# The attention half of a sketched-attention and expert-layer kernel, rebuilt

## The chip, the core and the metric

The kernel runs on one core of a Trainium2 chip. A core has the matrix engine TensorE (PE, with its weight loads shown apart as PEld), VectorE (DVE), ScalarE (ACT), GpSimd (POOL) and a queue SyncE (SP) that issues DMAs; they run side by side and meet at semaphores. The metric is device microseconds of one execution, the median of several. All arithmetic is fp32; each fp32 matmul shows in the trace as two pairs of a weight load (LDWEIGHTS) and a MATMUL, a transpose as one pair.

## What is computed

```python
# q, k, v: (B, H, S, D) = (4, 4, 1088, 32); S1, S2: (r, D) = (8, 32), float64 on arrival
def phi(x):
    a = np.einsum('rd,bhsd->bhsr', S1, x)
    b = np.einsum('rd,bhsd->bhsr', S2, x)
    return np.einsum('bhsi,bhsj->bhsij', a, b).reshape(*x.shape[:-1], r * r)
q_p, k_p = phi(q), phi(k)
kv  = np.einsum('bhsf,bhsd->bhfd', k_p, v);   z = np.sum(k_p, axis=2)
x   = np.einsum('bhsf,bhfd->bhsd', q_p, kv) / (np.einsum('bhsf,bhf->bhs', q_p, z)[..., None] + 1e-06)
x   = x.transpose(0, 2, 1, 3).reshape(4352, 128)            # one row per token
logits = x @ w_gate                                         # 8 experts
e_idx  = argmax(logits); gate_w = softmax(logits)[e_idx]; eom = sigmoid(x @ w_output_gate)
out[t] = gate_w[t] * eom[t, e] * (relu(x[t] @ w1[e]) @ w2[e])     # e = e_idx[t], 128 -> 1024 -> 128
```

## The kernel before

Tokens lie in 34 chunks of 128, and chunks in nine groups of four (the last has two). The work has two halves.

**Attention and routing.** For a group of keys, `ab` (L253) multiplies each chunk and pair of heads with both sketches: the chunk of `kT` is the stationary operand (128 columns), `S12blk` the moving one (32 columns). The sketches arrive as float64 and are held as a high and a low fp32 part, so `kT` and `qT` are loaded twice, once for each part, into partitions 0 to 63 and 64 to 127. ScalarE copies the b half out of PSUM (L256) and VectorE forms all products a·b (`kp`, L259). `kvs` (L280) sums `kp` against `vt` over the tokens of one batch entry, 65 moving columns (64 values and a one for z); `fin` (L266, L269) masks the result into `kz`. A batch entry has 1088 tokens, 8.5 chunks, so some chunks are split. For a group of queries, `fa` and `fb` (L298) compute features times tokens directly with 512 moving columns, ScalarE copies one (L305), VectorE multiplies (L310), `nd` (L318) multiplies with `kz` (66 moving columns: numerators and denominators), VectorE divides (L321 to L325), and `logits` transposes x (L333) and multiplies with the gate matrix (L338, 16 moving columns). `route` (L357 to L400), once a group, finds the winning expert, counts places with two matmuls (L372, L373), forms the gate weight, and then GpSimd writes each chunk's rows with one scatter (L400) to the place of its expert in the DRAM array `xs`: 34 scatters. The order of this half comes from a scheduler that places instructions by their dependences. At its end GpSimd writes one scatter of padding rows (L446), and VectorE makes a table of the 41 tiles of 128 rows (L451 to L484).

**Experts.** Each of the 41 tiles is read back from `xs` (L496), transposed (L507), multiplied up (L516) and down (L526) with the weights of its expert, scaled and scattered to the output (L529). This half has an order written by hand and is not touched. Its first read must wait until all scatters into `xs` have landed.

PSUM tiles come from rings: "t" and "w2" have two buffers each, "kvz" and "rt" one.

Of the kernel before, what the change touches and what calls it, by code (L numbers as in the profile page):

```python
# [2 lines left out]

# [8 lines left out]
F32 = mybir.dt.float32  # L12
# [18 lines left out]
def kernel(  # L31
# [52 lines left out]
    rows = consts.tile([2 * r, 128], F32, tag="rows")  # L84
    bits = consts.tile([2 * r, 64, 2], I32, tag="bits")
    if not wide:
        nc.vector.memset(rows, 0.0)
    for i, x in enumerate((S1, S2)):
        own = slice(i * r, (i + 1) * r)
        if wide:  # L90
            x, dst, n = x.bitcast(I32), bits[own].rearrange("p (h d) w -> p h (d w)", h=2), 2 * D
        else:
            dst, n = rows[own, :64].rearrange("p (h d) -> p h d", h=2), D
        nc.sync.dma_start(dst, bass.AP(tensor=x.tensor, offset=x.offset, ap=[[n, r], [0, 2], [1, n]]))
    wg = consts.tile([DM, 2 * E], F32, tag="wg")
    nc.sync.dma_start(wg, wg_d)
# [3 lines left out]
    kT = consts.tile([128, 2, N], F32, tag="kT")  # L100
    qT = consts.tile([128, 2, N], F32, tag="qT")
# [6 lines left out]
    def load_T(dst, src, g):  # L108
        cs = groups[g]
        for i in range(2):  # L110
            nc.sync.dma_start(dst[64 * i:64 * (i + 1), :, cols(cs)],
                              src[:, cols(cs)].rearrange("(a p) n -> p a n", a=2))

    def load_k(g):
        cs = groups[g]
        load_T(kT, kT_d, g)
# [3 lines left out]
    def load_q(g):  # L120
        load_T(qT, qT_d, g)
# [12 lines left out]
    lead = need[0] + 1  # L134
    for g in range(lead):
        load_k(g)
# [16 lines left out]
    make_identity(nc, ident)  # L153
    ones = consts.tile([128, 128], F32, tag="ones")
# [8 lines left out]
    nc.vector.tensor_scalar(efirst, eio, -1.0, float(E), op0=ALU.mult, op1=ALU.add)  # L163
    ecap = consts.tile([128, E], F32, tag="ecap")
    nc.vector.tensor_scalar_mul(ecap, eio, float(CAP))
# [16 lines left out]
    nc.vector.tensor_copy(padoff, padoff_i)  # L182
    padcap = consts.tile([128, E], F32, tag="padcap")
    nc.vector.tensor_scalar_mul(padcap, eio, float(CAP - PP * PR))
# [5 lines left out]
    nc.vector.tensor_copy(step, step_i)  # L190
    stepT = consts.tile([128, max(NT, KN)], F32, tag="stepT")
    nc.vector.tensor_scalar_mul(stepT, step, float(TS))  # L192
# [5 lines left out]
    def split():  # L198
# [3 lines left out]
        sign, ex, mant, low, scale = (consts.tile([2 * r, 64], I32, tag=f"bit{i}", name=f"bit{i}") for i in range(5))  # L202
# [11 lines left out]
        nc.vector.tensor_copy(rows[:, :64], mant.bitcast(F32))  # L214
        nc.vector.tensor_copy(rows[:, 64:], low)
        nc.vector.tensor_mul(rows[:, 64:], rows[:, 64:], scale.bitcast(F32))
    if wide:
        split()

    ps = ps_t("ps_rows")  # L220
    nc.tensor.transpose(ps[:, :2 * r], rows, ident[:2 * r, :2 * r])
    S12T = consts.tile([128, 2 * r], F32, tag="S12T")
    nc.vector.tensor_copy(S12T, ps[:, :2 * r])

    mask2 = consts.tile([128, 2], F32, tag="mask2")
    maskh = consts.tile([128, 2], F32, tag="maskh")
    nc.vector.memset(maskh, 0.0)
    for h in range(2):
        nc.vector.memset(maskh[64 * h:64 * (h + 1), h:h + 1], 1.0)
    nc.vector.memset(mask2, 0.0)  # L230
    for i in range(4):
        nc.vector.memset(mask2[i * D:(i + 1) * D, i % 2:i % 2 + 1], 1.0)

    S12blk = consts.tile([128, 2, 2 * r], F32, tag="S12blk")
    nc.vector.tensor_mul(S12blk, bview(S12T, [[0, 2], [1, 2 * r]]), bview(mask2, [[1, 2], [0, 2 * r]]))
# [5 lines left out]


    kvz_done, acc = {}, {}

    def k_steps(g):
        cs, s = groups[g], {}
        n = len(cs) * H
# [345 lines left out]
```

## Time and profile before

| | us |
|---|---|
| median of three runs | 307.65 (306.43 to 311.29) |
| the profiled execution's own time | 307.44 |
| its span, first to last instruction | 305.7 |
| PE busy, PEld busy | 265.9, 243.1 |
| DVE, POOL, ACT busy | 103.3, 77.5, 57.5 |

A busy time counts the stretch in which an engine has at least one instruction in flight. Matmuls are pipelined, so the time from one start to the next says more than the length of one. The chain of waits is followed back from the last instruction to what released each step; the table of stages gives the busy time of each engine in chosen stretches.

### The profile page before, as it was taken

How to read it: one execution, taken by the hardware profiler on the slowest of the kernel's cores; microseconds unless marked ns; L12 is line 12 of the kernel's file. 1: busy time of each engine (PE TensorE's matmuls, PEld its weight loads, DVE VectorE, ACT ScalarE, POOL GpSimd, SP SyncE). 2: the span in 40 equal slices, each digit the busy share in tenths (PEclk: the TensorE clock that was granted, in tenths of full speed). 3: DMA queues.
4: the chain of work that ended last, by engine and by line, in shares of the span. 5: the costliest groups of instructions: out<-in, count | busy, mean ns of one | idle time of the engine just before them, and what ended most of it. 6: DMA issues, size and time to landing. Idle time of an engine off the chain costs nothing.

```text
span 305.7 us, 5829 instructions
## 1 busy us (share of the span) xinstructions
PE 265.9 (87%) x1990; PEld 243.1 (80%) x1990; DVE 103.3 (34%) x402; ACT 57.5 (19%) x108; POOL 77.5 (25%) x108
## 2 busy tenths in 40 slices
PE   0997979999999988402999999999999999999980
PEld 0996557787786657402999999999999999999980
DVE  5202115555665655761222222222222222222200
ACT  1000102121122121100122222222222222222220
POOL 4000000235135134770022222222222222222230
PEclk9999979899999999655899999999999999999997
DMA  5999999601011001112158488878783288751000
GB/s 137 248 239 248 238 240 294 246 26 35 2 36 38 9 27 37 45 56 76 35 171 260 152 242 244 253 234 288 208 288 116 71 247 244 233 201 37 17 2 0
DMA packets 22062, 44.50 MB, mean 146 GB/s; under 512 B 3642, under 2 KB 9532, under 8 KB 22032
## 3 DMA queue, kind: packets, MB, share of 16 engines
q1 hardware_dynamic: 19488, 39.10, 45.6%
q0 software_dynamic: 2544, 5.03, 4.8%
q8 instruction: 16, 0.26, 0.4%
q14 instruction: 14, 0.11, 0.1%
HBM read 60.06 MB, written 5.48 MB: 214 GB/s over the span
## 4 chain that ended last, share of the span: by engine, by line
issue 39%; PE 35%; POOL 13%; DVE 4%; DMA 3%; POOLq 1%; ACT 1%; SPq 1%; ACTq 0%
POOL out_dram L529 12%; PE ps_kvz L280 7%; PE ps_ab L253 6%; PE ps_fa L298 6%; PE ps_nd L318 6%; PE ps_fb L298 4%; PE ps_l L338 3%; DMA kT<-in_k_dram 1%; DMA xs<-pad,pai 1%; PE ps_xt L333 1%; POOLq L529 1%; PE ps_pos L372 1%; DVE kp L259 1%; DMA xin<-xs 1%; PE ps_pos L373 1%
## 5 line engine op out<-in xcount | busy, mean ns | idle before, releaser
L516 PE MATMUL ps_h<-xsT,wt 128*128 128x128 f32 x656 | 81.8, 279 | 0.0
L526 PE MATMUL ps_y<-wt,hT 128*128 128x128 f32 x656 | 79.8, 275 | 0.0
L516 PEld LDWEIGHTS ps_h<-xsT,wt 128*128 128x128 f32 x656 | 78.4, 196 | 0.0
L526 PEld LDWEIGHTS ps_y<-wt,hT 128*128 128x128 f32 x656 | 76.5, 192 | 0.0
L529 POOL DMA_INDIRECT out_dram<-y,xin x41 | 39.8, 971 | 122.0 <-ACT y L528 122.0
L400 POOL DMA_INDIRECT xs<-x,sloti x34 | 33.3, 981 | 98.2 <-DVE sloti L390 63.3
L509 DVE COPY xsT<-ps_xs 128x128 f32<-128x128 f32 x41 | 12.0, 292 | 86.8 <-PE ps_xs L507 86.8
L520 DVE TENSOR_SCALAR hT<-ps_h 128x1024 f32<-128x1024 f32 x20 | 24.5, 1225 | 30.1 <-PE ps_h L516 21.1
L518 ACT ACTIVATE hT<-ps_h 128x1024 f32<-128x1024 f32 x21 | 21.5, 1023 | 50.9 <-PE ps_h L516 28.7
L528 ACT ACTIVATE y<-ps_y,xin 128x128 f32<-128x128 f32 x41 | 15.1, 367 | 81.1 <-PE ps_y L526 81.1
L280 PEld LDWEIGHTS ps_kvz<-vt,kp 128*128 128x128 f32 (+1 forms) x144 | 23.5, 245 | 8.1 <-DVE kp L259 4.4
L280 PE MATMUL ps_kvz<-vt,kp 128*128 128x65 f32 (+1 forms) x144 | 24.0, 330 | 3.8 <-DVE kp L259 3.2
L507 PE MATMUL ps_xs<-ident,xin 128*128 128x128 f32 x41 | 11.7, 286 | 14.3 <-DMA xin<-xs 14.3
L253 PEld LDWEIGHTS ps_ab<-S12blk,kT 128*128 128x128 f32 x136 | 20.8, 241 | 2.6 <-DVE stepT L192 2.1
L253 PE MATMUL ps_ab<-S12blk,kT 128*128 128x32 f32 x136 | 20.9, 316 | 2.0 <-DMA kT<-in_k_dram 2.0
L298 PE MATMUL ps_fa<-qT,Sa 128*128 128x512 f32 (+1 forms) x36 | 21.9, 728 | 0.0
L318 PEld LDWEIGHTS ps_nd<-kz,qp 128*128 128x128 f32 (+1 forms) x144 | 16.7, 187 | 2.1 <-issue 1.5
L318 PE MATMUL ps_nd<-kz,qp 128*128 128x66 f32 (+1 forms) x144 | 18.1, 274 | 0.1
L259 DVE TENSOR_TENSOR kp<-ps_ab,b_sb 128x1024 f32<-128x1024 f32 (+1 forms) x9 | 10.5, 1165 | 22.3 <-ACT b_sb L256 20.2
L507 PEld LDWEIGHTS ps_xs<-ident,xin 128*128 128x128 f32 x41 | 6.0, 148 | 14.7 <-DMA xin<-xs 14.7
L298 PE MATMUL ps_fb<-qT,Sb 128*128 128x512 f32 (+1 forms) x36 | 16.9, 591 | 0.0
L310 DVE TENSOR_TENSOR qp<-a_sb,ps_fb 128x1024 f32<-128x1024 f32 (+1 forms) x9 | 10.4, 1160 | 12.1 <-PE ps_fb L298 11.6
(117 smaller groups left out, 146.6 us busy)
## 6 DMA issues: line engine op xcount, KB each, us to landing
wt<-in_w_dram SPq DMA_DIRECT2D x88, 512.0 KB
kT<-in_k_dram SPq DMA_DIRECT2D x16, 256.0 KB
qT<-in_q_dram SPq DMA_DIRECT2D x16, 256.0 KB
xin<-xs SPq DMA_DIRECT2D x41, 65.0 KB
vt<-in_v_dram SPq DMA_DIRECT2D x8, 260.0 KB
out_dram<-y,xin POOLq DMA_INDIRECT x41
xs<-x,sloti POOLq DMA_INDIRECT x34
kT<-in_k_dram SPq DMA_DIRECT2D x2, 128.0 KB
```

Source lines behind the costliest of these rows:

```text
L253: nc.tensor.matmul(ps[:, j * H + 2 * p:j * H + 2 * p + 2], kT[:, p, c * 128:(c + 1) * 128], S12blk, start=True, stop=True)
L280: nc.tensor.matmul(acc[b][:, p], s["kp"][p0:p0 + np_, j * H + 2 * p:j * H + 2 * p + 2].rearrange("s h i j -> s (h i j)"), vt[p0:p0 + np_, ...
L298: nc.tensor.matmul(ps[:, p, :n], S_.rearrange("p h i j -> p (h i j)"), qT[:, p, cols(cs)], start=True, stop=True)
L318: nc.tensor.matmul(ps[p0:p0 + np_, p, j], s["qp"][:, p, j * 128 + p0:j * 128 + p0 + np_], kvz_done[b][:, p], start=True, stop=True)
L400: apart("rows", nc.gpsimd.indirect_dma_start(out=xs[:, :], out_offset=bass.IndirectOffsetOnAxis(ap=sloti[:, j:j + 1], axis=0), in_=s["x"][ ...
L507: nc.tensor.transpose(ps, xin[t][:, :DM], ident)
L516: nc.tensor.matmul(ps[:, c], wt[t % NW][0][:, c], xT, start=True, stop=True)
L518: nc.scalar.activation(hTs[t], ps, ACTF.Relu)
L520: nc.vector.tensor_scalar_max(hTs[t], ps, 0.0)
L526: nc.tensor.matmul(ps, hT[:, c], wt[t % NW][1][:, c], start=(c == 0), stop=(c == FC - 1))
L528: nc.scalar.activation(y, ps, ACTF.Copy, scale=x[:, DM:DM + 1])
L529: apart("out", nc.gpsimd.indirect_dma_start(out=out, out_offset=bass.IndirectOffsetOnAxis(ap=x.bitcast(I32)[:, DM + 1:DM + 2], axis=0), in ...
```

## The change

The expert half stays. In the attention half:

- `kT` and `qT` hold each value once (128 rows: four heads of 32). The high and low parts of the sketches become two matmuls that add up in PSUM.
- Keys and queries go through the same `featured`: per chunk four matmuls with 64 stationary columns (half a chunk of tokens) and 64 moving ones, into the upper and the lower half of the PSUM partitions in turn; then the same copy and the same product as before for keys. `fa`, `fb` and L310 go.
- `sums` has one matmul for each head (64 stationary columns), halves in turn. `turned` transposes the query products, two transposes a chunk, and ScalarE copies them. `attend` has four matmuls a chunk with 64 stationary columns and 98 moving ones: the 66 of before and 32 more that hold `kz` times the gate matrix (`gates_T`, `gates`, once a batch entry). `shared` divides and adds up the logits on VectorE, so the transposes, matmuls and copies of `logits` go.
- Routing is done for eight chunks at once (`choose`, `place`, `send`): five times, of 8, 8, 8, 8 and 2 chunks. Places are counted with a scan; two small operations of it go to GpSimd. There are still 34 scatters and one of padding.
- The loads are issued as a list of 18 items: k0 k1 k2 q0 k3 q1 k4 q2 k5 q3 k6 q4 k7 q5 k8 q6 q7 q8. A loop over n = 0 to 21 writes out the order by hand: `featured` of item n, `place`, `sums` or `turned` of item n-1, `gates_T`, `attend` of item n-2, `gates`, `send`, `shared`, `choose`.
- Constants for routing are made on GpSimd instead of VectorE, and the gate matrix is loaded behind the first key group.

```diff
-    kT = consts.tile([128, 2, N], F32, tag="kT")
-    qT = consts.tile([128, 2, N], F32, tag="qT")
+    kT = consts.tile([128, N], F32, tag="kT")
+    qT = consts.tile([128, N], F32, tag="qT")
...
-        load_T(kT, kT_d, g)
+        nc.sync.dma_start(kT[:, cols(cs)], kT_d[:, cols(cs)])
...
+    items, made = [], 0
     for g in range(len(groups)):
-        load_q(g)
-        if lead + g < len(groups):
-            load_k(lead + g)
+        while made < len(groups) and made < max(need[g] + 1, need[0] + 1 + g):
+            items.append(("k", made))
+            made += 1
+        items.append(("q", g))
+    wg2 = consts.tile([2 * D, 2, 2 * E], F32, tag="wg2")
+    for i, (kind, g) in enumerate(items):
+        (load_k if kind == "k" else load_q)(g)
+        if i == 0:
+            nc.sync.dma_start(wg2, wg_d.rearrange("(s p) e -> p s e", s=2))
...
+    carry = consts.tile([128, E], F32, tag="carry")
+    nc.gpsimd.memset(carry, 0.0)
+    nc.gpsimd.tensor_copy(carry[0:1], ecap[0:1])
+    RG = 2 * GRP // 128
+    routes = [range(c, min(c + RG, NC)) for c in range(0, NC, RG)]
...
+    Sb = consts.tile([128, 2, H, 2 * r], F32, tag="Sb")
+    nc.vector.tensor_mul(Sb, bview(ps, [[2 * r, 2], [0, H], [1, 2 * r]]), bview(maskh, [[0, 2], [1, H], [0, 2 * r]]))
...
+    def featured(src, cs, name):
         n = len(cs) * H
+        ps = ps_t("ps_ab")[:, :4 * H * 2 * r].rearrange("p (a b) -> p a b", b=2 * r)
+        for j, c in enumerate(cs):
+            for i in range(2):
+                for t in range(2):
+                    nc.tensor.matmul(ps[64 * t:64 * (t + 1), j * H:(j + 1) * H],
+                                     src[:, c * 128 + 64 * t:c * 128 + 64 * (t + 1)], Sb[:, i],
+                                     start=i == 0, stop=i == 1, skip_group_check=True)
+        b_sb = work.tile([128, 4 * H, r], F32, tag="b_sb", name="b_sb")
+        nc.scalar.copy(b_sb[:, :n], ps[:, :n, r:])
+        res = work.tile([128, 4 * H, r, r], F32, tag=name, name=name)
+        av, bv = ps[:, :n, :r], b_sb[:, :n]
+        nc.vector.tensor_mul(res[:, :n], ...)
...
+    def gates_T(b):
+        ps = psum.tile([2 * D, 2, 128], F32, tag="rt", name="ps_kzT")
+        for s in range(2):
+            nc.tensor.transpose(ps[:, s], kz[b][:, s, :2 * D], ident)
+        kzT = work.tile([2 * D, 2, 128], F32, tag="kzT", name="kzT")
+        nc.scalar.copy(kzT, ps)
+        return kzT
+    def gates(b, kzT):
+        ps = psum.tile([128, 2, 4 * E], F32, tag="rt", name="ps_kg")
+        for s in range(2):
+            nc.tensor.matmul(ps[:, s], kzT[:, s], wgb[:, s].rearrange("p h e -> p (h e)"), start=True, stop=True)
+        nc.scalar.copy(kz[b][:, :, VZ:], ps)
+    def sums(cs, kp, todo):
...
+                for s in range(2):
+                    for h in range(2):
+                        nc.tensor.matmul(acc[b][64 * h:64 * (h + 1), s],
+                                         kp[p0:p0 + np_, j * H + 2 * s + h].rearrange("s i j -> s (i j)"),
+                                         vt[p0:p0 + np_, c, s], start=first and s == 0, stop=last, skip_group_check=True)
+                if last:
+                    close(b)
+                    todo.append(b)
+                    yield
+    def turned(cs, qp):
+        n = len(cs)
+        ps = ps_w("ps_qT").rearrange("p a (c x) -> p (a c) x", x=128)
+        for j in range(n):
+            for s in range(2):
+                nc.tensor.transpose(ps[:, 2 * j + s], qp[:, j * H + 2 * s:j * H + 2 * s + 2].rearrange("p h i j -> p (h i j)"), ident)
+        qpT = work.tile([128, 8, 128], F32, tag="qpT", name="qpT")
+        nc.scalar.copy(qpT[:, :2 * n], ps[:, :2 * n])
+        return qpT
+    def attend(cs, qpT):
+        ps = ps_w("ps_nd").rearrange("p a (c x) -> p (a c) x", x=128)
+        for j, c in enumerate(cs):
+            for s in range(2):
+                for t in range(2):
+                    nc.tensor.matmul(ps[64 * t:64 * (t + 1), 2 * j + s, :VG], qpT[:, 2 * j + s, 64 * t:64 * (t + 1)],
+                                     kz[(c * 128 + 64 * t) // S][:, s], start=True, stop=True)
+        return ps
+    def shared(cs, ps):
...
+        nc.vector.tensor_scalar_add(rc_, ps[:, :2 * n, 2 * D:VZ], EPS)
+        nc.vector.reciprocal(rc_, rc_)
+        nc.vector.tensor_mul(xts[i][:, at:at + n, :DM]..., ps[:, :2 * n, :2 * D]..., rc_...)
+        lg = work.tile([128, 8, 2, 2 * E], F32, tag="lg", name="lg")
+        nc.vector.tensor_mul(lg[:, :2 * n], ps[:, :2 * n, VZ:VG]..., rc_...)
+        nc.vector.tensor_reduce(Ls[i][:, at:at + n], lg[:, :2 * n]..., axis=AX, op=ALU.add)
...
+    def choose(i):
...
+        nc.vector.tensor_reduce(mx[:, :n], L, axis=AX, op=ALU.max)
+        nc.vector.tensor_tensor(ex[:, :n, :E], bc(mx), L, op=ALU.subtract)
+        nc.vector.scalar_tensor_tensor(out=t8[:, :n], ...)
+        nc.vector.tensor_reduce(first[:, :n], t8[:, :n], axis=AX, op=ALU.max)
+        nc.scalar.copy(oh[:, :, 0], state["carry"])
+        nc.vector.tensor_tensor(oh[:, :, 1:]..., t8[:, :n], bc(first), op=ALU.is_equal)
+        nc.vector.tensor_tensor_scan(cum..., fresh[n]..., oh..., 0.0, op0=ALU.mult, op1=ALU.add)
+    def place(i, oh, cum):
+        pp = psum.tile([128, E, RG], F32, tag="rt", name="ps_pos")[:, :, :n]
+        nc.tensor.matmul(pp, before, oh[:, :, 1:], start=True, stop=False)
+        nc.tensor.matmul(pp, ones, cum[:, :, :n], start=False, stop=True)
+    def send(i, oh, pp):
...
+        nc.vector.tensor_tensor(t9[:, :n], oh_, G, op=ALU.mult)
+        nc.vector.tensor_reduce(gs[:, :n], t9[:, :n], axis=AX, op=ALU.add)
+        nc.scalar.activation(ex[:, :n, E + 1], gs[:, :n], ACTF.Relu, scale=-1.0)
+        nc.scalar.activation(ex[:, :n, E + 2], gs[:, :n], ACTF.Abs)
+        nc.scalar.activation(ey[:, :n], ex[:, :n], ACTF.Exp, scale=-1.0)
+        nc.vector.tensor_tensor(t10[:, :, :n], pp, oh[:, :, 1:], op=ALU.mult)
+        nc.vector.tensor_reduce(sloti[:, :n], ...)
+        nc.vector.tensor_reduce(ss[:, :n], ey[:, :n, :E + 1], axis=AX, op=ALU.add)
+        nc.vector.scalar_tensor_tensor(out=co[:, :n], ...)
+        nc.vector.reciprocal(co[:, :n], co[:, :n])
+        nc.gpsimd.tensor_copy(x.bitcast(I32)[:, :n, DM + 1], ids[:, routes[i][0]:routes[i][-1] + 1])
+        nc.gpsimd.tensor_mul(x[:, :n, DM], co[:, :n], ey[:, :n, E + 1])
+        for j in range(n):
+            apart("rows", nc.gpsimd.indirect_dma_start(...))
...
+    with tc.manual_schedule():
+        prods, turns, chosen = {}, {}, None
+        todo, gateT = [], []
+        for n in range(len(items) + 4):
+            kind, g = items[n] if n < len(items) else (None, None)
+            if kind:
+                prods[n] = featured(kT if kind == "k" else qT, groups[g], kind + "p")
+            placed = None
+            if chosen:
+                placed = chosen + (place(*chosen),)
+                chosen = None
+            ready, todo = todo, []
+            fills = None
+            if 0 <= n - 1 < len(items):
+                kind, g = items[n - 1]
+                if kind == "k":
+                    fills = sums(groups[g], prods.pop(n - 1), todo)
+                    next(fills, None)
+                else:
+                    turns[n - 1] = turned(groups[g], prods.pop(n - 1))
+            gateT = [(b, gates_T(b)) for b in ready]
+            ps = None
+            if n - 2 in turns:
+                g = items[n - 2][1]
+                ps = attend(groups[g], turns.pop(n - 2))
+            if fills:
+                for _ in fills:
+                    pass
+            for b, kzT in gateT:
+                gates(b, kzT)
+            if placed:
+                send(placed[0], placed[1], placed[3])
+            if ps is not None:
+                shared(groups[g], ps)
+                for i, rs in enumerate(routes):
+                    if rs[-1] == groups[g][-1]:
+                        chosen = (i,) + choose(i)
```

## Rows read from the trace of the kernel before

**Rows 1.** Stages: length, engines' busy us (instructions), granted clock, DMA share, GB/s
```profile
0.00:7.15 7.15, 0.26 (x1) 0.20 (x2) 3.96 (x36) 1.28 (x1) 3.28 (x32) 1.00 0.52 127
7.15:14.16 7.01, 7.01 (x33) 7.01 (x34) 1.22 (x1) 0.27 (x1) 0.00 (x0) 1.00 1.07 254
56.00:124.30 68.30, 64.38 (x426) 50.59 (x424) 41.39 (x220) 14.62 (x33) 24.64 (x26) 1.00 0.10 36
130.00:141.50 11.50, 0.00 (x0) 0.00 (x0) 5.37 (x22) 0.00 (x0) 5.29 (x6) 0.50 0.23 81
148.20:297.50 149.30, 148.80 (x1333) 148.61 (x1332) 35.68 (x59) 36.15 (x62) 38.82 (x40) 1.00 0.59 181
```
**Rows 2.** Chain of waits: start, length, what held the end
```profile
1.63 0.36 SPq L96
...
2.80 4.22 DMA kT<-in_k_dram
7.15 7.01 PE ps_ab L253 x32
...
42.38 3.41 PE ps_fa L298 x4
...
61.59 0.44 PE ps_xt L333 x4
62.03 1.71 PE ps_ab L253 x16
63.74 0.88 PE ps_l L338 x8
64.62 1.81 PE ps_fa L298 x4
66.43 1.73 PE ps_kvz L280 x16
...
135.75 3.87 DMA xs<-pad,pai
139.63 1.82 DMA xin<-xs
```
**Rows 3.** Tile ps_nd alone: length, PE, PEld, DVE, granted clock, DMA, GB/s
```profile
68.50:68.89 0.39, 0.39 (x8) 0.32 (x8) 0.00 (x0) 1.00 0.00 0
107.13:107.48 0.35, 0.35 (x5) 0.31 (x4) 0.00 (x0) 1.00 0.00 0
69.00:70.22 1.22, 1.22 (x12) 1.22 (x12) 0.00 (x0) 1.00 0.00 0
```
**Rows 4.** TensorE in order of time: start, length, engine, line, operation
```profile
68.19 0.39 PE L373 MATMUL ps_pos<-cnt,ones 128*128 128x32 f32 x2
68.51 0.46 PE L318 MATMUL ps_nd<-kz,qp 128*64 128x66 f32 x8
```
**Rows 5.** Groups by line and shape, first 150 us: busy, mean ns, idle before
```profile
L259 DVE TENSOR_TENSOR kp<-ps_ab,b_sb 128x1024 f32<-128x1024 f32 x8 | 9.8, 1225 | 22.0 <-ACT b_sb L256 20.2 <-issue 1.8
...
L305 ACT COPY a_sb<-ps_fa 128x1024 f32<-128x1024 f32 x8 | 8.1, 1012 | 23.0 <-PE ps_fa L298 23.0
...
L325 DVE TENSOR_TENSOR x<-ps_nd,rc 128x256 f32<-128x256 f32 x16 | 6.3, 420 | 0.1
...
L256 ACT COPY b_sb<-ps_ab 128x128 f32<-128x128 f32 x8 | 2.1, 265 | 29.6 <-PE ps_ab L253 29.6
...
L383 ACT ACTIVATE ex<-ex 128x40 f32<-128x40 f32 x8 | 1.9, 238 | 4.8 <-DVE ex L381 3.4 <-DVE cnt L367 1.1 <-DVE cnt L369 0.3
...
L357 DVE TENSOR_REDUCE mx<-L 128x4 f32<-128x32 f32 x8 | 1.4, 181 | 5.1 <-ACT L L340 5.1
```
**Rows 6.** GpSimd in order of time, first and last of eight scatters
```profile
122.79 0.97 POOL L400 DMA_INDIRECT xs<-x,sloti  x1 [3.91 <-DVE rc L322]
...
131.72 0.97 POOL L400 DMA_INDIRECT xs<-x,sloti  x1 [0.30 <-issue]
```
**Rows 7.** DMA issues of the page: queue, count, KB each
```profile
kT<-in_k_dram SPq DMA_DIRECT2D x16, 256.0 KB
```

More of the change, by code (lines that the diff above doesn't have):

```diff
@@ L83 @@
     wide = S1.dtype != F32
[L84 to L87, printed above, removed]
+    rows = [consts.tile([2 * r, H, D], F32, tag=f"rows{i}", name=f"rows{i}") for i in range(2)]
+    bits = consts.tile([2 * r, D, 2], I32, tag="bits")
+    plain = consts.tile([2 * r, D], F32, tag="plain")
     for i, x in enumerate((S1, S2)):
@@ L153 @@
     make_identity(nc, ident)
+    maskh = consts.tile([128, H], F32, tag="maskh")
+    nc.vector.memset(maskh, 0.0)
+    for h in range(H):
+        nc.vector.memset(maskh[h * D:(h + 1) * D, h:h + 1], 1.0)
+    maskr = consts.tile([128, 2], F32, tag="maskr")
+    nc.vector.memset(maskr, 0.0)
+    for i in range(2):
+        nc.vector.memset(maskr[64 * i:64 * (i + 1), i:i + 1], 1.0)
     ones = consts.tile([128, 128], F32, tag="ones")
@@ L201, in split, with heads @@
         lo, hi = bits[:, :, 0], bits[:, :, 1]
-        sign, ex, mant, low, scale = (consts.tile([2 * r, 64], I32, tag=f"bit{i}", name=f"bit{i}") for i in range(5))
+        sign, ex, mant, low, scale = (consts.tile([2 * r, D], I32, tag=f"bit{i}", name=f"bit{i}") for i in range(5))
+        def heads(t):
+            return t.unsqueeze(1).to_broadcast((2 * r, H, D))
         nc.vector.tensor_scalar(sign, hi, 31, 31, op0=SHR, op1=SHL)
@@ L220 @@
     ps = ps_t("ps_rows")
[L221 to L232, printed above, removed]
@@ L405 @@
-    made = 0
-    def keys(upto):
-        nonlocal made
-        while made < min(upto, len(groups)):
-            for f in k_steps(made):
-                f()
-            made += 1
-    keys(lead)
-    prev = None
-    for g in range(len(groups) + 1):
-        now = q_steps(g) if g < len(groups) else None
-        if now:
-            now[0]()
-        if prev:
-            keys(need[g - 1] + 1)
-            prev[2]()
-        if now:
-            now[1]()
-        if prev:
-            prev[3]()
-        keys(lead + g + 1)
-        if prev:
-            prev[4]()
-        prev = now
+    for i in range(2):
+        nc.tensor.transpose(ps[:, 2 * r * i:2 * r * (i + 1)], rows[i].rearrange("p h d -> p (h d)"), ident[:2 * r, :2 * r])
@@ new lines, in sums @@
+    def sums(cs, kp, todo):
+        for j, c in enumerate(cs):
+            for b, p0, np_ in parts(c):
+                first, last = c * 128 + p0 == b * S, c * 128 + p0 + np_ == (b + 1) * S
+                if first:
+                    acc[b] = psum.tile([128, 2, HV], F32, tag="kvz", name="ps_kvz")
+                for s in range(2):
[7 more added lines that the diff above has]
+                    yield
@@ L433 @@
     pn = psum.tile([128, E], F32, tag="rt", name="ps_n")
-    nc.tensor.matmul(pn, ones, seen["tile"][:, seen["at"]], start=True, stop=True)
+    nc.tensor.matmul(pn, ones, state["carry"], start=True, stop=True)
     num = consts.tile([128, E], F32, tag="num")
-    nc.vector.tensor_copy(num, pn)
+    nc.vector.tensor_sub(num, pn, ecap)
     pd = consts.tile([128, E], F32, tag="pd")
```

265 lines of the change are left out of this document (95 added, 170 removed).

## The prediction

> **What bounds the kernel now.** I read the stages first. From 148.20 us on, TensorE is busy in 148.80 of 149.30 us [rows 1]; that is the expert half, which the change doesn't touch. In 56 to 124.3 it is busy in 64.38 of 68.30 us while VectorE has 41.39 and GpSimd 24.64 [rows 1]: the attention half is bound by TensorE too. Between 130.00 and 141.50 TensorE does nothing [rows 1]; the chain shows what it waits for: the padding scatter, issued at 135.75, lands 3.87 later, the first read of `xs` takes 1.82, and the experts start at 141.5 [rows 2]. So the end is set by TensorE, then GpSimd's queue of scatters, then TensorE. From 141.5 to the end of the span are 164.2 us, and the profiled execution is 1.7 us longer than its span. These 166 us I leave as they are; the question is when the padding scatter is issued. Every us by which that moves, the whole moves.
>
> What TensorE does in the attention half is in the chain. `ab` takes 1.71 for 16 records (0.107 each) with 32 moving columns, `l` 0.88 for 8 (0.110) with 16, `kvz` 1.73 for 16 (0.108) with 65; only `fa`, with 512, takes 0.452 [rows 2]. Thin matmuls thus cost what loading 128 stationary columns costs. That is the waste which 64-column matmuls address. At the start the same `ab` took 7.01 for 32, 0.219 each [rows 2]: half speed. The granted clock reads 1.00 there [rows 1], but the step is that of the 1.2 GHz level; the column isn't to be trusted ahead of its first change.
>
> **Price of a 64-column record.** The trace has 16, where a chunk is split between two batch entries. With one half alone (107.13) four weight loads take 0.31 us of TensorE's time; with both halves together (68.50) eight take 0.32, the eight records 0.39, and twelve of full width behind them 1.22 [rows 3]. The halves run side by side. Those eight begin with a slow first step; for a long run I take half of the full-width step, 0.055, and a little, 0.058 for a record in each half at once. Bounds: 0.029 for each record if the overlap holds in long runs, 0.058 if it doesn't (the lone half). The eight are the nearest row, so I take the overlap. A group of four chunks then costs:
> - F (`featured`): 16 matmuls, 32 records, 16 a half: 16 x 0.058, with 0.07 to start, 1.0 us.
> - S (`sums`): the same, 1.0.
> - A (`attend`): 98 moving columns at `fa`'s 0.452 for 512 [rows 2] are 0.087 a record; 16 a half, 1.45.
> - T (`turned`): 8 transposes at 0.11 (`xt`, 0.44 for four [rows 2]), 0.9, and two changes between full and half width. Such a change shows where `pos` ends: the second of its two records starts 0.11 behind 68.19, the next, half-width one at 68.51 [rows 4], some 0.1 more than a step. T is 1.1.
> - `place` is 4 records, 0.5; `gates` 2 transposes and 2 matmuls, 0.7 with copies between.
>
> The Trainium skill has a rule against this: "TensorE: Matmul & The Clock Gate", section "Wait — 56ns, not 53.3ns?", says that with hardware decode off each MATMUL takes some 62 ns to issue, which binds when the array's work is shorter. By it F, S and A would be 2.0 each; the eight records in 0.39 us, 0.049 each, are under that, but a queue filled ahead could hide it in so short a run. That is the first rival below.
>
> **The other engines.** VectorE: a product stays 1.225; one is added for each query group in place of L310. `shared` is two small ones of 0.2, x of 512 elements 0.69 (between 0.42 for 256 and 1.225 for 1024), `lg` and its sum 0.42 each: 2.0. `choose` is six operations of about 0.22 (0.18 for 32 elements [rows 5]), 1.4; the scan has no row and lies between 0.2 and the 0.42 of 256 elements. `send` is seven small ones, 1.6. ScalarE: b_sb 0.265, the copy of `turned` 1.0 as a_sb, activations 0.24 [rows 5]. GpSimd: a scatter every 1.276 us (122.79 to 131.72, seven steps [rows 6]). Its two new small operations have no row: from 0.1 each (32 instructions in 3.28 us [rows 1]) to the 0.97 of a scatter; I take the low side, 0.4 together. They stand ahead of the scatters in its queue and wait for the gate weight, so all eight scatters now wait for it. Constants moved to GpSimd cost nothing: its setup is 3.28 us before 7.15 [rows 1], and the first of them is needed near 30 us; without that cover they would be about ten at 0.1 to 0.97. Loads: each key piece was two DMAs of 256 KB [rows 7]; now it is one. DMA moved 254 GB/s [rows 1], so the first piece lands 1.0 us earlier, and the gate matrix, 0.36 of SyncE's time ahead of it [rows 2], is moved behind it: TensorE starts at 5.7 instead of 7.15. The loads keep their order otherwise. A key and a query group now take 3.2 us to load, less than any pair of steps below, so later loads are hidden; if they weren't, TensorE would wait for each.
>
> **The sum.** Start 5.7. TensorE is at half speed at first: F, F, S cost 6, then F, S, F, S about 4.8: 16.5 at the end of step 3. Step 4 is F, T, `gates`: 3.4, 19.9. Step 5 is F, S, A: 3.45, 23.4.
>
> Then a loop closes that I follow from the end of one A to the next. VectorE's queue is in order: `shared` 2.0, then the next key product 1.2, and only then can S start; TensorE has F, T, F (3.1) to do meanwhile. So S starts 3.4 after A, and S and A make 5.9 for a key and a query group.
> Where a routing falls due, `place` sits in TensorE's queue behind F and waits for `choose`: 2.0 + 1.4 + 0.1 = 3.5. Behind it are T (at 5.2), `gates`, whose transposed `kz` is copied behind the 1.0 copy of T on ScalarE (6.5), the gate matmuls (7.0), F, S, A: 10.4 for this pair. Its `send` waits on ScalarE behind the same copies: exponentials at 7.9, the weight at 8.4, GpSimd's first scatter 8.8 after A.
> From 23.4: pair 29.3, routing pair 39.7, pair 45.6, routing pair 56.0, a pair with the half group k8 4.8: 60.8. The third `send` starts scatters at 69.6; eight last to 79.8. The fourth is ready at about 78.7 (60.8 + 17.9: two more A, `shared`, `choose`, `send`), so GpSimd goes straight on: 0.4 and ten scatters, 12.8, padding at 93.0. TensorE idles in each routing pair, and the clock may fall there. `fa` at 42.38 shows the price, 3.41 us against 1.81 [rows 2]; I add 1.7 for each of the two routing pairs on this path, 3.4: 96.4.
> The padding scatter moves from 135.75 to 96.4, so the time is 307.4 - 39.4 = **268.0 us**. The run profiled lies 0.2 under the median of the runs; I make nothing of that. VectorE's table, most of its 5.37 us in 130 to 141.5 [rows 1], is made while GpSimd still scatters.
>
> **Rivals.**
> *The halves don't overlap in long runs, or the issue limit binds.* For: only eight records show the overlap. Then F and S are 1.9, A 2.8; the start takes until 33.9, a pair 9.6, a routing pair 13.6, a half pair 7.2: 87.5 in place of 60.8; the fourth `send` is ready at 109.1, padding at 121.9: 13.9 gained, **293.5**.
> *The clock stays at 1.2 GHz.* For: `ab` ran at half speed from 7.15 to 14.16 though TensorE was busy in all of it [rows 1, 2], and `fa` again at 42.38. Against: 56 to 124.3 has 1.00 granted with `ab`, `l` and `kvz` between the long ones [rows 1, 2]. All TensorE steps double: a pair 10.9, a routing pair 15.7, the last A of the loop at 94.3, padding at 132: **303.6**, which is no change.
> *Slower: each change of half drains the array.* 552 matmuls now change half at nearly each one. The overlap lost leaves 13.9 us, so 13.9 / 552 = 0.025 us a change is enough to be slower than before; at the 0.1 of a change of width [rows 4] it is 55 us, **349**. Against: the eight records at 68.50 took 0.39 us, no more than one half alone. In the Trainium skill, "TensorEngine Tiling (Array Packing)", section "Key Properties", only a change of mode, not of tile, drains; rows 3 agree.
> *GpSimd binds from the first scatter.* If the steps run closer than I have them, 34 scatters and padding go without a gap from 38.1: 43.4 and 0.8, padding at 82.3: **254**. That is the floor, since no step shortens the scatters.
>
> **How the numbers follow.** Forecast with its stalls somewhat longer or shorter, down to the floor: 0.70 (its own range 254 to 280). No overlap or partly: 0.13. Clock low throughout or for half of it (303.6, or about 286): 0.12. Draining halves: 0.03. Others, such as a lasting wait between engines: 0.02. The range reaches from the floor, less 2 us for shorter waits, up to 292: it takes in the forecast, partial overlap and the mixed clock, some 0.8. A measurement of this kernel can tell about 2% from no change. Faster by more (under 301.5): 0.70 + 0.13 + half of 0.12 and a little, 0.90; within 2%: 0.06; slower: 0.04.
>
> **What would show it.** `ps_ab` with 64 rows by 64 columns of output at some 0.03 us a record; the first scatter at 38 to 40 us, scatters 1.28 apart within a routing and gaps between the first three; `place` waiting for VectorE; the padding scatter near 96 and the experts' first transpose 5.75 later, with 164 us behind it. It is wrong if the records of `featured` stand 0.06 or more apart, if the granted clock is 0.5 through the attention half, if TensorE waits mostly for something that the loop above doesn't have, or if scatters are slower in rows of eight.

## The result, and the profile after

The changed kernel takes 271.9 us (median of four runs, 271.7 to 273.0) against 307.1 for the kernel before: a ratio of 0.888, 95% interval 0.884 to 0.891. On a second chip it was 272.4, 0.889 (0.882 to 0.895). The forecast was 268.0 in a range of 252 to 292. Some executions take a few per cent longer, most of them at a lower granted clock (of the kernels below one once took 430.9 us, the kernel before once 545.4); the ratios leave these out.

The stages after: length, busy us of PE, PEld, DVE, ACT and POOL (instructions), granted clock, DMA share, GB/s. They are the start, the loads, the part up to the first send, the sends up to the padding, the gap, the experts.
```profile
0.00:6.14 6.14, 0.40 (x2) 0.32 (x2) 3.52 (x27) 1.28 (x1) 5.14 (x45) 1.00 0.50 150
6.14:17.39 11.25, 9.64 (x239) 9.29 (x240) 5.17 (x6) 1.06 (x4) 0.43 (x5) 1.00 1.04 381
17.39:41.29 23.90, 19.46 (x408) 17.83 (x406) 14.16 (x31) 6.18 (x17) 0.21 (x1) 0.93 0.51 199
41.29:99.72 58.43, 34.76 (x584) 30.26 (x578) 38.89 (x122) 11.21 (x34) 35.81 (x42) 0.79 0.12 39
99.72:105.42 5.70, 0.02 (x1) 0.02 (x1) 0.00 (x0) 0.00 (x0) 0.97 (x1) 0.50 0.32 117
105.42:270.00 164.58, 154.14 (x1353) 153.65 (x1353) 36.47 (x61) 36.58 (x62) 39.88 (x41) 0.96 0.54 165
```
Before, TensorE was busy in 64.4 of 68.3 us of the attention half [rows 1]. Now it is busy in 34.8 of the 58.4 us between the first send and the padding, and no engine is busy throughout: the stage is a chain that changes hands. The expert half is what it was, 164.6 us (164.2 before).

The chain of waits after (start, length, what held the end), from the first sketch to the experts:
```profile
2.49 3.14 DMA wg<-in_wg_dram
5.66 0.23 DVE wgb L259
6.14 3.68 PE ps_ab L274 x64
11.30 0.93 PE ps_ab L274 x32
14.45 1.23 DVE qp L281
17.39 1.52 PE ps_ab L274 x32
18.90 1.91 PE ps_qT L331 x8
20.84 1.01 ACT qpT L333
21.85 0.27 ACT kzT L300
...
29.99 1.38 PE ps_nd L341 x32
...
33.57 0.23 DVE mx L377
...
35.16 0.41 PE ps_pos L394 x2
...
35.91 0.89 PE ps_qT L331 x8
36.83 1.01 ACT qpT L333
...
70.26 1.06 PE ps_kg L306 x4
71.32 1.05 PE ps_ab L274 x16
72.37 1.90 PE ps_qT L331 x8
74.27 2.12 PE ps_nd L341 x32
...
97.12 0.34 POOL xs L422
...
99.72 3.72 DMA xs<-pad,pai
103.46 1.90 DMA xin<-xs
```
A sketch product of 32 half-width records takes 0.93 us at the full clock; one of 16 full-width records took 1.71 [rows 2]. At 18.90 and 72.37 eight transposes take 1.9 us, at 35.91 they take 0.89: the first two are at 1.2 GHz (granted clock 0.50 there, 1.00 at 35.91). The padding is sent 36.0 us earlier than before [rows 2].

### The profile page after: what moved, and what is told of

Read it like the earlier page. It is cut to its first block, busy times and chain, and to the rows that moved or that the text cites. A ratio compares the mean times of both kernels' runs of the same rounds, so it can differ in the third digit from the quotient of the medians.

```text
span 270.0 us, 6822 instructions
## 1 busy us (share of the span) xinstructions
PE 218.4 (81%) x2573; PEld 211.4 (78%) x2573; DVE 98.2 (36%) x246; ACT 56.3 (21%) x118; POOL 82.4 (31%) x132
## 4 chain that ended last, share of the span: by engine, by line
issue 44%; PE 18%; POOL 16%; DVE 11%; DMA 3%; ACT 2%; POOLq 2%; SPq 1%; DVEq 0%
POOL out_dram L563 14%; PE ps_nd L341 5%; PE ps_ab L274 4%; PE ps_kvz L318 3%; PE ps_qT L331 3%; DVE x L356 2%; ACT qpT L333 2%; POOL xs L422 2%; DVE L L362 2%; DMA xs<-pad,pai 1%; DMA wg<-in_wg_dram 1%; POOLq L563 1%; PE ps_kg L306 1%; DVE kp L281 1%; DVE lg L360 1%
## 5 line engine op out<-in xcount | busy, mean ns | idle before, releaser
L422 POOL DMA_INDIRECT xs<-x,sloti x34 | 34.2, 1006 | 11.6 <-issue 8.5
L341 PE MATMUL ps_nd<-kz,qpT 128*64 128x98 f32 x272 | 14.6, 263 | 0.7 <-ACT qpT L333 0.7
L420 POOL TENSOR_TENSOR x<-co,ey 128x8 f32<-128x8 f32 (+1 forms) x5 | 1.0, 209 | 45.3 <-DVE co L418 45.3
L341 PEld LDWEIGHTS ps_nd<-kz,qpT 128*64 128x64 f32 x272 | 13.0, 147 | 1.4 <-ACT qpT L333 0.9
L318 PE MATMUL ps_kvz<-vt,kp 128*64 128x65 f32 (+1 forms) x288 | 11.7, 229 | 2.6 <-DVE kz L292 1.6
L281 DVE TENSOR_TENSOR kp<-ps_ab,b_sb 128x1024 f32<-128x1024 f32 (+1 forms) x9 | 10.4, 1155 | 7.4 <-ACT b_sb L278 7.4
L394 PE MATMUL ps_pos<-oh,before 128*128 128x64 f32 (+1 forms) x10 | 2.6, 343 | 12.8 <-DVE oh L384 12.8
L318 PEld LDWEIGHTS ps_kvz<-vt,kp 128*64 128x64 f32 (+1 forms) x288 | 10.1, 142 | 3.6 <-issue 1.7
L394 PEld LDWEIGHTS ps_pos<-oh,before 128*128 128x128 f32 x10 | 1.9, 237 | 13.7 <-DVE oh L384 11.5
L333 ACT COPY qpT<-ps_qT 128x1024 f32<-128x1024 f32 (+1 forms) x9 | 8.7, 965 | 18.0 <-PE ps_qT L331 18.0
L278 ACT COPY b_sb<-ps_ab 128x128 f32<-128x128 f32 (+1 forms) x18 | 4.7, 260 | 36.9 <-PE ps_ab L274 36.6
```

The costliest lines, as they stand in the source:

```text
L281: nc.vector.tensor_mul(res[:, :n], bview(av, [list(av.ap[1]), list(av.ap[2]), [0, r]]), bview(bv, [list(bv.ap[1]), [0, r], list(bv.ap[2])]))
L318: nc.tensor.matmul(acc[b][64 * h:64 * (h + 1), s], kp[p0:p0 + np_, j * H + 2 * s + h].rearrange("s i j -> s (i j)"), vt[p0:p0 + np_, c, s] ...
L333: nc.scalar.copy(qpT[:, :2 * n], ps[:, :2 * n])
L341: nc.tensor.matmul(ps[64 * t:64 * (t + 1), 2 * j + s, :VG], qpT[:, 2 * j + s, 64 * t:64 * (t + 1)], kz[(c * 128 + 64 * t) // S][:, s], sta ...
L422: apart("rows", nc.gpsimd.indirect_dma_start(out=xs[:, :], out_offset=bass.IndirectOffsetOnAxis(ap=sloti[:, j:j + 1], axis=0), in_=x[:, j] ...
```

## The experiments

The first four kernels ran on one chip and came out above what either theory gave them: the order of the halves by 7 us, the others by 18 to 34. The changed kernel and three of the four were then run on other chips. Line numbers in the rows of an experiment are its own.

**Full width.** The 64-column matmuls are undone; the rest stays.
```
-            for t in range(2):
-                nc.tensor.matmul(ps[64*t:64*(t+1), j*H:(j+1)*H], src[:, c*128+64*t:c*128+64*(t+1)], Sb[:, i], ...)
+            nc.tensor.matmul(ps[:, j*H:(j+1)*H], src[:, c*128:(c+1)*128], Sb[:, i], ...)
```
(the same in `sums` and `attend`).

> One part undone: the matmuls of featured, sums and attend have 128 stationary columns again (half as many matmuls, same data, same order), all else as changed. Theory A (the two halves load their weights side by side, and that is where TensorE's time went): a record of featured and of sums stands 0.107 us behind the last and not 0.029, so featured and sums of a group take 1.7 and not 0.93 us, attend 1.75 and not 1.38; a pair of a key and a query group 7.8 and not 5.4, and the whole about 290 us (287 to 294). Theory B (the gain is from fewer operations, less loading and routing by eight chunks, and the halves add little): 272 to 276 us.

Measured: 327.5 us (320.8 to 338.1; the trace is of one of 325.9). On another chip:

> The 128-column matmuls again (one record for both halves in the sketches, the kvz sums and the nd products, everything else as in the changed kernel), on another chip than the first time. The first trace showed something that neither theory had: with 128-column records the first sketch product of 16 records took 3.2 us and so did every later one up to 57 us, at 1.2 GHz, and 1.7 us from 61 us on; in the changed kernel 32 records of 64 columns take 0.93 us from 11 us on. Theory A (width alone: the two halves run side by side, so a full-width record costs as much as the four half-width ones that it replaces take twice over, and the clock rises when it does in the changed kernel): 287 to 295 us. Theory E (width and clock: with 128-column records TensorE stays at 1.2 GHz until past 50 us whatever the chip, some 26 us more): 305 to 322 us, and the trace has F at 3.2 us until past 50 us again.

Measured: 324.7 us (306.1 to 334.7, at mean granted clocks of 0.932 and 0.846; the profiled run is the one at 334.7). Groups by line in two stretches of that trace, 8 to 50 us and 61 to 65 us (count, busy us, mean ns of one):
```profile
L273 PE MATMUL ps_ab<-Sb,kT 128*128 128x64 f32 x57 | 12.8, 421 | 0.0
...
L273 PE MATMUL ps_ab<-Sb,kT 128*128 128x64 f32 x16 | 1.9, 275 | 0.0
```
The trace is as theory E has it, on both chips: the records start 0.21 us apart until 56 us, the step of 1.2 GHz, and 0.11 apart from there, that of 2.4. TensorE was not idle in between: from 6.2 to 27 us it was busy throughout, from 27 to 50 in 21.1 of 23.0 us. Of the times only the shortest lies in theory E's range. By the end of the second nd product the kernel is 28.4 us behind the changed one (59.8 against 31.4). Its TensorE had some 41 us of work after the first sketches at 1.2 GHz; at 2.4 GHz that is 20 less, so by this estimate about 20 of the 28.4 are clock and 8 are width.

The execution of 306.1 us left no trace. By the two mean clocks it spent about 41 us at the lower level behind the first change of its records, the traced one about 102. 61 us more at half speed cost some 30, and the times differ by 28.6: later falls of the clock are enough to explain that, but whether its clock too rose at 56 us is not shown. Even this one takes what the kernel before takes: as far as one execution shows it, the rest of the change gains nothing without the half-width records.

**Order of the halves.** All of the lower half first, then all of the upper.
```
-        for j, c in enumerate(cs):
-            for i in range(2):
-                for t in range(2):
+        for t in range(2):
+            for j, c in enumerate(cs):
+                for i in range(2):
```
(the same in `sums` and `attend`)

> Same 64-column matmuls, other order: in each group all matmuls of the lower half first, then all of the upper half, instead of in turn. Theory A (TensorE looks only a few records ahead, so the halves overlap only if they alternate closely): featured and sums take up to 1.9 us each, attend 2.75; a pair 9.4, the whole about 300 us (290 to 304). Theory B (each half works through its own records however they are queued): nothing changes, 271 to 273 us.

Measured: 311.0 us (309.3 to 312.3), ratio 1.003 (0.999 to 1.008). On another chip:

> The 64-column matmuls with all of the lower half first and then all of the upper half, again, on another chip. In the first trace a sketch product took about 1.5 us between 13 and 42 us, against 0.93 in the changed kernel, and the first send came at 49.0 us against 41.3, before any of the idle gaps that made up the rest of its 311 us. Theory A (the order of the halves is what sets them side by side; the part that the gaps added is gone): 281 to 291 us. Theory B (64 columns are enough and the order does nothing once the gaps are gone): 271 to 274 us.

Measured: 290.1 us (289.1 to 293.3, without the execution of 430.9), ratio 0.956 (0.943 to 0.969): theory A. TensorE in order of time, this kernel, then the changed one (start, length to the last end, line, form, count):
```profile
11.09 1.73 PE L322 MATMUL ps_kvz<-vt,kp 128*64 128x65 f32 x29
12.60 0.27 PE L274 MATMUL ps_ab<-Sb,kT 128*64 128x64 f32 x1
12.65 0.22 PE L322 MATMUL ps_kvz<-vt,kp 128*64 128x65 f32 x1
...
12.82 1.50 PE L274 MATMUL ps_ab<-Sb,kT 128*64 128x64 f32 x26
```
```profile
11.13 1.10 PE L274 MATMUL ps_ab<-Sb,kT 128*64 128x64 f32 x32
12.07 1.10 PE L318 MATMUL ps_kvz<-vt,kp 128*64 128x65 f32 x32
```
Within a block of one half the records start 0.052 us apart (29 from 11.09 to 12.60); only where the last records of one product meet the first of the next, in the other half, do the two alternate. In the changed kernel they start 0.029 apart (32 from 11.13 to 12.07). So it is the neighbour in the other half that is worth 0.023 us a record, and some 18 us in all (against 272.4, on another chip).

**Nine routings of four chunks.**
```
-    RG = 2 * GRP // 128
+    RG = GRP // 128
```


> One part undone: routing for four chunks at once (nine times) and not for eight (five times). Theory A (each routing holds TensorE, whose place matmuls stand in the queue ahead of the transposes and wait for VectorE's choose): the three pairs that had no routing take 8.5 us and not 5.4; the first scatter comes earlier, at about 34 us, the padding scatter later, near 106; the whole 276 to 281 us. Theory B (GpSimd's scatters set the end from the first of them on): the earlier first scatter wins, 34 scatters at 1.29 and nine heads of 1.0 us from 34 us on, the whole about 262 to 268 us.

Measured: 305.2 us (304.5 to 305.7), ratio 0.986 (0.977 to 0.994), on the first chip; what it is worth undisturbed is seen below, with other edits.

**Late placement.** `place` goes behind the gate block, so that nothing of TensorE stands behind it while VectorE chooses.
```
-            if chosen:
-                placed = chosen + (place(*chosen),)
...
             for b, kzT in gateT:
                 gates(b, kzT)
+            if chosen:
+                placed = chosen + (place(*chosen),)
```


> Order only: in each step the place matmuls stand behind the transposes, attend and gates on TensorE and no longer right behind featured. Theory A (in the steps with routing TensorE waits with place for VectorE while the transposes behind it could run, and ScalarE's copies follow late): a routing pair takes 8.2 to 8.6 us and not 10.8, the first scatter of a routing comes 7.9 us behind its attend and not 9.9; the padding scatter moves from 99.7 to about 91 to 93, the whole 263 to 266 us. Theory B (TensorE's own work or GpSimd's scatters set the end whatever the order): 271 to 273 us.

Measured: 290.9 us (289.0 to 291.9), ratio 0.937 (0.927 to 0.947). Up to 42 us its trace is as expected. Then TensorE in order of time shows this (in brackets the idle time ahead):
```profile
41.74 0.76 PE L274 MATMUL ps_ab<-Sb,kT 128*64 128x64 f32 x19
42.90 0.36 PE L274 MATMUL ps_ab<-Sb,kT 128*64 128x64 f32 x5 [0.40 <-issue]
43.63 0.35 PE L274 MATMUL ps_ab<-Sb,kT 128*64 128x64 f32 x5 [0.37 <-issue]
44.39 0.33 PE L274 MATMUL ps_ab<-Sb,kT 128*64 128x64 f32 x3 [0.41 <-issue]
```
Bursts of a few records, and idle time that no semaphore explains, until GpSimd's eight sends are done. Either the chip did this or the order of work. So the changed kernel and this one were run side by side on a second chip:

> The changed kernel, unaltered, beside the kernel before. The four variants that ran so far (one with 128-column matmuls, one with the halves one after the other, one with nine routings, one with the placement after the gate block) each came out 20 to 30 us above what either theory gave them, and in the traces of three of them TensorE stands idle with no wait shown, in gaps of 0.3 to 1.1 us, while GpSimd's row sends run. Theory C (this lies with the chip on which they ran): where such gaps come, the changed kernel has them too and its time is 285 to 300 us. Theory D (the gaps belong to the variants' order of work): the changed kernel is at 271 to 274 us and its trace has no such gaps between 41 and 68 us.

> The placement after the gate block, as run before (290.9 us then), now beside the changed kernel on the same chip. Theory C (the chip): it moves with the changed kernel, 263 to 268 us if the changed kernel is at 272, 285 to 292 if that has gaps too. Theory D (the order of work): 288 to 293 us again while the changed kernel is at 271 to 274.

Measured: 272.4 us (271.8 to 272.9) for the changed kernel, and 268.5 (266.8 to 270.7), ratio 0.874 (0.867 to 0.880), for the late placement. The same stretch of the late placement on the first and on the second chip (columns as in the table of stages):
```profile
42.90:51.00 8.10, 4.26 (x32) 2.50 (x33) 2.03 (x5) 0.00 (x0) 5.25 (x7) 0.80 0.15 50
```
```profile
42.60:51.00 8.40, 7.65 (x156) 6.68 (x154) 7.08 (x17) 2.51 (x6) 5.42 (x7) 1.00 0.16 50
```
TensorE did 156 records where it had done 32, beside the same sends. Theory C holds for this kernel: 22 us of its first time go with that chip, or with the hour, since it did not run there again. What made TensorE starve there stays open; the changed kernel itself did not run on it, and the kernel before was little touched (310.2 us against 306.7). The times of the first four kernels are therefore not compared with the forecast; their traces up to the first send are.

Against the changed kernel beside it the late placement gains 3.9 us, where 6 to 9 were expected. Its first three sends come 2.1, 2.2 and 3.1 us earlier, the fourth 2.0, the padding 1.3: the later sends have further waits behind this one. The traced execution is the longest of its four (270.7 us), 1.1 below that of the changed kernel; the 3.9 are the difference of the medians.

**The start.** wgb and the fills of `pad` are issued behind the first sketch product.
```
-    nc.gpsimd.memset(pad, 0.0)
-    nc.gpsimd.memset(pad.bitcast(I32)[:, :, DM + 1], NOWHERE)
...
-    nc.vector.tensor_mul(wgb, ...)
...
                 prods[n] = featured(...)
+            if n == 0:
+                nc.vector.tensor_mul(wgb, ...)
+                nc.gpsimd.memset(pad, 0.0)
+                nc.gpsimd.memset(pad.bitcast(I32)[:, :, DM + 1], NOWHERE)
```


> Two edits at the start alone: the product that makes wgb and the two fills of pad are issued after the first sketch product, not before the loop. In the changed kernel two integer operations of VectorE take 1.07 and 0.99 us beside GpSimd's 0.96 us fill of pad, against 0.16 to 0.20 us for their neighbours, and the product for wgb waits until 5.63 us for its transfer with Sb behind it. Theory A (both are on the way to the first sketch matmul and all that follows hangs on it): the first ps_ab starts at 4.9 to 5.2 us instead of 6.14, the integer operations take about 0.2 us, and the time falls by 0.8 to 1.3 us. Theory B (something later decides, a load of k or a wait of the first sends): the first ps_ab is earlier but the time is the same within 0.3 us.

Measured: 271.4 us (270.5 to 274.9) beside 272.4. VectorE in order of time, the changed kernel and this one:
```profile
3.34 1.07 DVE L229 TENSOR_SCALAR bit<-bit 16x32 int32<-16x32 int32 x1
3.43 0.99 DVE L232 TENSOR_TENSOR bit<-bit,bit 16x32 int32<-16x32 int32 x1
```
```profile
3.34 0.17 DVE L227 TENSOR_SCALAR bit<-bit 16x32 int32<-16x32 int32 x1
3.43 0.17 DVE L230 TENSOR_TENSOR bit<-bit,bit 16x32 int32<-16x32 int32 x1
```
The first `ps_ab` starts at 5.01 us instead of 6.14 (6.37 in the second trace of the changed kernel), and the first send comes at 40.28 instead of 41.27. But the second send comes at 58.90, 1.3 later than there: in this trace the granted clock fell at 36 us (0.58 in 35 to 40 us), where the changed kernel has 1.00. The median fell by 1.0, the two ranges of runs overlap, and the traced execution is 1.3 longer, not shorter. So the cause of the late start is shown, but the gain in time that theory A gives is not clear of the noise.

**Shorter routings, and GpSimd's small operations.** Both with the start and the late placement.
```
-    RG = 2 * GRP // 128
+    RG = GRP // 128
```


> Three edits together: the start (first ps_ab at 5.0 us), the placement after the gate block, and nine routings of four chunks in the place of five of eight. With the first two alone the sum is 267 to 268 us: 268.5 measured for the late placement, less about 1 us of the start. Theory A (GpSimd's 43.5 us of sends is the train that ends last, and it starts at 39 us and stands idle for 14 us between its runs of eight; four chunks a routing start it at about 33 us and fill most of the idle time): 261 to 265 us. Theory B (each of the four further routings costs TensorE, VectorE and ScalarE about as much on the way to the last product as it saves GpSimd): 267 to 272 us.

Measured: 270.8 us (269.1 to 272.4), ratio 0.888 (0.879 to 0.898): theory B, and at the slow end of it. The sends start at 32.2 us, but there are now nine placements, and TensorE waits for VectorE's choice in six of them, 12.7 us in all, against 7.0 in two in the next kernel. The start and the late placement with eight chunks and nothing else did not run; their 267 to 268 us are a sum.
```
-        nc.gpsimd.tensor_copy(x.bitcast(I32)[:, :n, DM + 1], ...)
-        nc.gpsimd.tensor_mul(x[:, :n, DM], co[:, :n], ey[:, :n, E + 1])
+        nc.vector.tensor_copy(...)
+        nc.vector.tensor_mul(...)
```


> The start and the late placement as in the kernel beside it, five routings of eight chunks, and the two small operations of a routing that GpSimd does ahead of its sends (the copy of the ids, 0.2 us, and the product for the coefficient, 0.2 us, after which the first send waits another 0.6 us) on VectorE. From about 71 us on GpSimd is busy or blocked nearly without a break over the last three routings. Theory A (these 0.8 to 1.0 us a routing are on GpSimd's train): 264 to 266 us, and a send follows the last product of its routing within 0.3 us. Theory B (the 0.6 us is a start-up of the send itself, whoever writes its rows): 267 to 268.5 us, and the wait is still there.

Measured: 263.0 us (262.2 to 265.9), ratio 0.861 (0.855 to 0.868). GpSimd in order of time in the changed kernel, then VectorE's last product and GpSimd's first send here:
```profile
56.86 0.21 POOL L420 TENSOR_TENSOR x<-co,ey 128x8 f32<-128x8 f32 x1 [5.16 <-DVE co L418]
57.66 1.03 POOL L422 DMA_INDIRECT xs<-x,sloti  x1 [0.59 <-POOL x L420]
```
```profile
68.83 0.17 DVE L417 TENSOR_TENSOR x<-co,ey 128x8 f32<-128x8 f32 x1
...
69.28 0.97 POOL L419 DMA_INDIRECT xs<-x,sloti  x1 [5.65 <-DVE x L417]
```
From the end of the product to the send are 0.28 us instead of 0.59: theory A, with 1 us more than its range gave. The 0.59 are not the price of every product of GpSimd's: in the changed kernel's fifth routing, where it came straight from its sends to the product, the send follows in 0.28 too (at 97.12 us). The longer gap shows where GpSimd had stood idle ahead of the product.

**Gates first.** To that kernel one more edit: the transposes of the closed kz go ahead of those of the query product.
```
+            gateT = [(b, gates_T(b)) for b in ready]
             fills = None
             if 0 <= n - 1 < len(items):
...
-            gateT = [(b, gates_T(b)) for b in ready]
```


> The start, the late placement and the two small operations on VectorE, as in the kernel at 263.0 us, and one thing more: the two transposes of the closed kz go ahead of the eight transposes of the query product, and ScalarE's copy of theirs (0.27 us) ahead of its copy of the queries' (1.01 us). In that kernel TensorE waits 1.14 us for the copy of kzT in each of four pairs, with the placement, the next sketch product and the next nd product behind it. Theory A (this wait is on the way to the three sends that follow, two of which GpSimd stands ready for): about 1 us at the second and third send each, the third send at 66 to 67 us against 69.28, and 259.5 to 261.5 us. Theory B (the choose and the product on VectorE are as late as the copy was, so the placement waits for them instead): 262 to 263.5 us.

Measured: 258.6 us (257.6 to 259.4), ratio 0.844 (0.840 to 0.849): theory A, and better than it. TensorE's waits in the kernel without this edit, then with it (us in total, times, longest):
```profile
PE ps_pos L391 <- DVE oh L381: 7.0, 2, 4.1
PE ps_kg L303 <- ACT kzT L297: 4.6, 4, 1.1
...
PE ps_pos L391 <- ACT kz L304: 0.6, 2, 0.3
...
PE ps_pos L391 <- issue: 0.3, 1, 0.3
```
```profile
PE ps_pos L391 <- DVE oh L381: 8.0, 3, 4.1
...
PE ps_pos L391 <- DVE cum L383: 0.7, 1, 0.7
...
PE ps_pos L391 <- ACT kz L304: 0.7, 1, 0.7
```
The 4.6 us for kzT are gone, and at the placement 9.4 us stand where 7.9 stood. The third send starts at 63.24 us, and from there GpSimd sends without a gap to the padding at 86.46. The two kernels ran on different chips; the intervals of their ratios to the kernel before do not overlap. This kernel is the best of the study, at 0.844 of the kernel before where the changed one is at 0.889. From the 254 us that the prediction worked out as the floor it is 4.6 away: its first send is 1.9 earlier than was taken there (36.2 against 38.1), and the two gaps that are left, 46.3 to 50.0 and 59.9 to 63.2 us, hold 6.4 beyond the 0.3 between any two sends.

## Why the prediction was right, and where its steps were off

**The bound: right.** The padding moved by 36.0 us and the profiled run by 35.4 (307.4 to 272.1). The experts start 5.70 us behind it (5.75 foreseen); what is lacking lies in the expert half (164.6 us, foreseen 164.2) and around the span (2.1, foreseen 1.7).

**The price of a record: right.** F, S and A are 0.93, 0.93 and 1.38 (1.0, 1.0, 1.45 foreseen), 0.029 us a record in F and S and 0.043 in A. Of the two sides of the bound, 0.029 is the long-run value with the halves alternating; halves in blocks cost 0.052, near the other bound of 0.058. The rival without overlap gave 293.5; the kernel that has none but at the seams took 290.1. The rival of a drain at each change of half is out by the same 0.029, with a change at every record. The rival of 0.06 us an issue is out: 32 records in 0.93 us are 0.029 each. The rule of the Trainium skill behind it ("TensorE: Matmul & The Clock Gate", section "Wait — 56ns, not 53.3ns?") does not bind here; the same section's other floor, about 25 ns from start to start however little a matmul does, allows the 0.029, which lies just above it.

**The clock: the right price, for a weaker reason than it needed.** The forecast took full speed from the third step on because `ab`, `l` and `kvz` ran so in 56 to 124 us. The full-width kernel shows that this alone was no ground: in both its traces the same work stayed at 1.2 GHz until 56 us. The trace of the kernel before has such a stretch too, in rows of its chain that the prediction did not read: 16 records of `ab` still took twice the time at 21 us.
```profile
21.04 3.37 PE ps_ab L253 x16
...
37.06 1.72 PE ps_ab L253 x16
```
That the half-width records leave that level at about 11 us is a gain of its own, and the forecast had it by assumption: here it was lucky.

**The start: off by 2.8 us.** The first nd product was to end at 23.4 and ended at 26.2. The gate matrix was held to be out of the way because its transfer was moved behind the first keys; but the product made from it was issued ahead of Sb on VectorE, and Sb ran some 0.2 us late. Two integer operations ended some 0.9 us late beside GpSimd's fill, which "cost nothing" had not foreseen. TensorE then waits 1.6 us (to 16.09) for VectorE to read a finished sum out of PSUM, which stands in VectorE's queue behind the first query product. Step 4 was entered at 3.4, though its terms F, T and `gates` add up to 2.8, and it took 5.4: a fall of the clock took the transposes from 0.9 to 1.9, and ScalarE's 1.01 us copy stood ahead of kzT's, which the prediction put into the routing pairs but left out here.

**The loop: right.** From the first nd product to the last of the loop 37.3 us were measured, 37.4 foreseen; pairs of 5.2, 5.7 and 4.9 (5.9, 5.9, 4.8), routing pairs of 10.8 and 10.7 (10.4). The waits are those that were named: VectorE's choice for the placement (2 us, which the late placement takes away), the copy of T ahead of kzT's (0.6 us in each routing pair, 1.1 in the kernels with the late placement; the last kernel takes it away).

**The send: 8.8 us from nd product to first send were 9.9.** The sum over the gate logits took 0.59 where 0.42 stood, and between GpSimd's product and its first send lie 0.6 us that had no row and no term.

**The fourth send: the step that failed.** GpSimd was to go straight on from the third to the fourth routing. It stood idle for 1.1 us before the fourth routing's product and sent 2.1 us after the third routing's end, because the fourth came 22.5 us after the last product of the loop instead of 17.9. Of these 4.6 us some 2.7 are the clock: between 70 and 76.4 us four pieces of TensorE's chain run at granted clocks of 0.5 to 0.7 (1.06 against 0.63 for the gate matmuls, 1.05 against 0.56 for half a group's sketches, 1.90 against 0.89 for T, 2.12 against 1.38 for A). Another 0.6 are the gap behind GpSimd's product; the rest was not traced to one cause. The 3.4 us that the forecast set aside for two falls of the clock were so about the right size, but it set them ahead of the third send, where the clock held; there they covered most of the 2.7 us that the last product of the loop came late and of the 1.5 of its send, so that the third send came at 73.9 where 73.0 stood. The total is 3.9 us over the forecast; 3.3 of them are the padding's, at 99.7 instead of 96.4. The errors that cancelled are larger than what is left.

## What to carry to other kernels

Thin fp32 matmuls should alternate between the two column halves record by record; here two halves in blocks lost most of the gain (0.956 against 0.888). A fall of the clock is hard to place in advance: in the changed kernel it fell behind waits of TensorE of 1.6 us (to 16.09) and 2.7 us (to 67.08) and held behind waits of 2.1 and 1.7 us (to 35.16 and 51.52), and in the kernel with the other start it fell behind the same wait of 2.1 us. So ask of a forecast what a fall at each wait would cost, and which sends it would delay. When no engine is busy throughout, read the waits of the in-order queues: the edits that gained most after the change moved one instruction past another or to another engine (a placement, a copy, two small operations ahead of the sends) and took no work away.

## What the runs showed of the hardware

- VectorE's integer operations on 16x32 elements took 1.07 and 0.99 us while GpSimd filled 1040 words a partition, and 0.17 without it; both ended within 0.03 us of the fill's end. In the Trainium skill, "SBUF — State Buffer", section "SBUF: two separate sides", the pair of ports that the two engines share is held for a whole instruction; the rows agree.
- The loads ran at 381 GB/s (6.14 to 17.39) where the kernel before had 254 [rows 1] with the same share of busy DMA. The pieces of k and q went from two DMAs of 64 partitions to one of 128; the full-width kernel has the higher rate too, so it is not TensorE's doing. No experiment took the DMAs alone.
- On one chip TensorE stood idle for up to 1.6 us at a time while row sends ran, in kernels that have no such gap on others. Its cause is open, and so is why TensorE left 1.2 GHz at 11 us with half-width records (those in blocks too: 0.052 us apart from 11.09) and at 56 with full-width ones.
